# Another order of the attention's steps behind the load of pair 12, in an attention and soft-MoE kernel

## The chip, the cores and the metric

One core of a Trainium2 chip runs the whole kernel as one program. The metric is the device time of one execution in microseconds (us), the median of several runs. One execution was also taken by the hardware profiler; its rows are used below.

## The reference

Inputs are q, k, v of 4 batches x 8 heads x 768 positions x 64, and the weights of a soft mixture of experts (8 experts, 4 slots each, 1024 hidden).

```python
scores = scale * q @ k.T - slopes * dist          # per head, ALiBi distance
scores = where(is_global | is_local, scores, -1e9) # 8 global keys, window of 96
a = softmax(scores); x = (a @ v) -> [3072 tokens, 512]
logits = x @ phi                                   # 32 slots
d = softmax(logits over tokens); slot_input = d.T @ x
slot_out[e] = relu(slot_input[e] @ w1[e]) @ w2[e]
c = softmax(logits over slots); out = c @ slot_out
```

## The kernel before

**Units.** The attention is done in 16 units u = 0 to 15, each a pair of heads (i = 0, 1) of one batch; four units make a batch. A unit's 768 positions are cut into 7 blocks of 120 keys; scores are held as keys by queries, with 216 queries a block. Everything of the attention is written as named steps, and the list `ORDER` (L55) names them in the order in which they are put into the program; `steps` (L888) maps names to functions. Each engine runs its own steps in the order of that list, and waits where a step's input, or the buffer it writes, isn't ready. So a change of `ORDER` changes each engine's queue and nothing else in the work.

**The steps of unit u**, with engine and line:
- `load_qk` (L424), `load_v` (L427): transfers, issued on SP. q and k of a unit go to `raw` (u % 2), v to half of `vt` (u % 2), so a load waits until unit u-2 has been read.
- `scores u k`, k = 0 to 2, on PE (L571), into one of two `sc` PSUM tiles; `biased u k` on VectorE (L580) adds the bias table, keeps a running maximum, and writes `tb` (u % 3).
- `max_t` (PE, L587) and `max_r` (VectorE, L592) make the maximum over the keys; `exponential u i` on ScalarE (L596).
- The weights are split into two f16 parts: `w_hi u i` on ScalarE (L599) writes the high part to `ph`; `w_lo u i part`, three parts, on GpSimd (L606), or `w_lo_dve` on VectorE, the rest. v is split the same way: `v_hi` on GpSimd (L539), `v_hi_act` on ScalarE (L542) or `v_hi_dve` on VectorE (L545), then `v_lo` on VectorE (L549).
- `values u i` on PE (L623): 39 f16 matmuls of 65 columns; the parts of `w_lo` are needed one after the other, the last one by the last 16 matmuls. It waits until the PSUM tile `x` of unit u-1 has been read.
- `ev_sums`, `ev_recs`, `ev_mul u i` on VectorE (L639, L645, L651): normalise into `xn`, of which there are three buffers, one for each two units. (The last unit has them head by head: `ev_sum`, `ev_rec`, L632, L636.)
- `tr u k` on PE (L663) transposes `xn`; `tr_copy u k` on ScalarE (L668) or `tr_copy_dve` on VectorE (L672) copies it out, 480 columns for k = 0 and 288 for k = 1; `logits u` on PE (L693) takes two units. `max_t`, `tr`, `logits`, `by_token` and `dispatch` share a ring of two PSUM banks.
- At the end of a batch: `logits_all` (VectorE, L710), `strip_max`, `strip_exp`, `strip_sum` (a running softmax over tokens: L727, L734 to L738, L744, L746), `by_token` (PE, L751), its copies (ScalarE, L764, L768), `dispatch` (PE, L774: 28 matmuls on `xn`), `dispatch_sum` (VectorE, L785).

**Weights.** The expert weights are 32 pieces of 1024 KB. Ten go to places of their own (`piece`, L413). Thirteen go to buffers of the attention, each of which is loaded by `free i` (L418) once its last reader in the attention is done. Which piece goes to which buffer follows from the order of the `free` steps in `ORDER` (`held`, L380 to L384); so does the order in which the nine `extra` steps, early in `ORDER`, load the unused ends of these buffers. One piece goes to `spot`; the last eight go to the first places again, in column halves, as the tail's first matmuls release them (L949 to L957). Up to eight transfers are under way at a time, issued in order.

**The tail.** Behind `ORDER`, `last_dispatch` (L802) finishes the softmax over tokens of the last batch, starting from `logits_all 15`; then the hidden layer (L104), the projections (L159) and the combination (L205) follow on PE, and copies (L218) and transfers bring the output out.

Of the kernel before, what the change touches and what calls it, by code (L numbers as in the profile page):

```python
# [28 lines left out]
QW = KB + WIN  # L29
# [278 lines left out]
def tile_attention_moe(ctx: ExitStack, tc: tile.TileContext, qk, v, phi, w1, w2, nn, out):  # L308
    nc = tc.nc
# [58 lines left out]
    phi_ = [t[:, 0:PH].bitcast(F16) for t in pht]  # L368
# [11 lines left out]
    held = []  # L380
    for name, i, *_ in ORDER:
        if name == "free":
# [70 lines left out]
    def blocks(w):  # L453
        return w[:, 0:6 * PB].rearrange("p (s c) -> p s c", c=PB)
# [19 lines left out]
    def late_constants():  # L474
        nc.gpsimd.tensor_tensor(out=i4, in0=ident[:, 0:32], in1=ident[:, 32:64], op=ALU.add)
        nc.gpsimd.tensor_tensor(out=i4, in0=i4, in1=ident[:, 64:96], op=ALU.add)
        nc.gpsimd.tensor_tensor(out=i4, in0=i4, in1=ident[:, 96:128], op=ALU.add)
        nc.gpsimd.tensor_copy(out=by_row.rearrange("p (s j) -> p s j", s=4), in_=ident.rearrange("p (s r) -> p s r", s=4)[:, :, 0:NS // 4])
        nc.gpsimd.memset(sl, 0.0)
        moe.constants()  # L480
# [18 lines left out]
    def tb(u):  # L499
        return tbuf[u % 3]  # L500
# [53 lines left out]
    def warm_x(u):  # L554
        for n in (256, 256, P):
            nc.tensor.matmul(out=xx[:, 0, 0:n], lhsT=idb[:, 0:P], rhs=idb[:, 0:n], start=True, stop=True)
# [31 lines left out]

    def max_r(u):
        m = ms.pop((u, "m"))[:, 0:P]  # L590
        nbs[u] = nb = wk.tile([P, 1], F32, name="nb", tag="nb", bufs=2)
        nc.vector.tensor_tensor_reduce(out=m, in0=m, in1=shift.to_broadcast([P, P]), scale=-T_SC, scalar=3.0e38, op0=ALU.add, op1=ALU.min, accum_out=nb)  # L592

    def exponential(u, i):
        t = tb(u)[:, i]
        nc.scalar.activation(out=t, in_=t, func=AF.Exp, bias=nbs[u], scale=T_SC)  # L596

    def w_hi(u, i):
        nc.scalar.copy(out=blocks(phi_[i])[:, :, 0:QW], in_=tb(u)[:, i].rearrange("p (s c) -> p s c", c=QW))  # L599

    def w_hi_dve(u, i):
        nc.vector.tensor_copy(out=blocks(phi_[i])[:, :, 0:QW], in_=tb(u)[:, i].rearrange("p (s c) -> p s c", c=QW))

    def w_lo(u, i, part, engine=None):
        c = slice(2 * part, 2 * part + 2)
        (engine or nc.gpsimd).tensor_tensor(out=blocks(plo_[i])[:, c, 0:QW], in0=tb(u)[:, i].rearrange("p (s c) -> p s c", c=QW)[:, c],  # L606
                                            in1=blocks(phi_[i])[:, c, 0:QW], op=ALU.subtract)

    def w_lo_dve(u, i, part):
        w_lo(u, i, part, nc.vector)  # L610

    def values(u, i):
        ph, pl = phi_[i], plo_[i]
        vh, vl = vhi[u % 2], vlo[u % 2]
        x = sums(u, i)
        ops = []
        for t in range(NJ):
            for j, c in ((t, PCOL[t]), (t - 1, PCOL[t - 1] + KB)):
                if j >= 0:
                    for w, vv, d in ((ph, vh, D + 1), (ph, vl, D), (pl, vh, D + 1)):  # L620
                        ops.append((t, c, w, vv, j, d))
        for z, (t, c, w, vv, j, d) in enumerate(ops):
            nc.tensor.matmul(out=x[:, (D + 1) * t:(D + 1) * t + d], lhsT=w[:, c:c + P], rhs=vv[:, j, i, 0:d],  # L623
                             start=(z == 0), stop=(z == len(ops) - 1), skip_group_check=True)
# [253 lines left out]

    def table_rest_act(u):
        table.rest(nc.scalar.copy)  # L880

    def table_pair_act(p):
        table.pair_act(p)

    def table_pair(p):
        table.pair(p)

    steps = dict(piece=piece_of, free=free, extra=extra, load_phis=load_phis, bcast=bcast, keys=keys, table_rest=table_rest, table_rest_act=table_rest_act, table_pair_act=table_pair_act, warm_x=warm_x, warm=warm,  # L888
                 table_even=table_even, table_odd=table_odd, table_pair=table_pair, load_qk=load_qk, load_v=load_v, v_hi=v_hi, v_hi_act=v_hi_act, v_hi_dve=v_hi_dve, v_lo=v_lo,
                 scores=scores, biased=biased, max_t=max_t, max_r=max_r, exponential=exponential, w_hi=w_hi, w_lo=w_lo, w_lo_dve=w_lo_dve, w_hi_dve=w_hi_dve,  # L890
                 values=values, ev_sum=ev_sum, ev_rec=ev_rec, ev_sums=ev_sums, ev_recs=ev_recs, ev_mul=ev_mul, tr=tr, tr_copy=tr_copy, tr_copy_dve=tr_copy_dve,
                 logits=logits, logits2=logits2, logits_half=logits_half, logits_all=logits_all, strip_max=strip_max, strip_exp=strip_exp,
                 strip_sum=strip_sum, by_token=by_token, by_token_copy=by_token_copy, lnat_copy=lnat_copy, dispatch=dispatch, dispatch_sum=dispatch_sum)
    late_constants()
    for name, u, *args in ORDER:
        steps[name](u, *args)
    left = LeftBanks()
    put_rest = last_dispatch(left, lambda: warm_x(last))
    att.close()


    tail = ExitStack()
# [327 lines left out]
```

## Time and profile before

| | us |
|---|---|
| median of 3 runs | 185.19 |
| lowest and highest run | 184.1 to 185.4 |
| the profiled execution, its own time | 184.54 |
| its span, first to last instruction | 182.5 |

The span is what the profile's times count from. PE is TensorE's matmul row, PEld its weight-load row, DVE is VectorE, ACT ScalarE, POOL GpSimd, SP the engine that issues transfers. Matmuls overlap in the pipeline, so PE's busy time can hold some waiting. `<-` in brackets behind a row tells how long the engine was idle before it and what ended that.

### The profile page before, as it was taken

What the parts mean: (1) busy time and instruction counts of PE and PEld (TensorE: products, weight loads), DVE (VectorE), ACT (ScalarE), POOL (GpSimd) and SP (SyncE); (2) the same over time, 40 slices, a digit from 0 to 9 for tenths busy, and PEclk for the clock granted to TensorE, in tenths of its full rate; (3) what the DMA queues carried; (4) which work ended last, traced back from release to release, by engine and by line L of the source; (5) the groups of instructions that cost most, each with busy time, mean ns of one, the idle gap of its engine ahead of it and who ended that gap; (6) DMA issues with size and microseconds to landing.
All of it is one profiled execution on the core that took longest, in us unless ns stands there. A gap on an engine that the chain in (4) does not pass through costs nothing.

```text
span 182.5 us, 6745 instructions
## 1 busy us (share of the span) xinstructions
PE 170.5 (93%) x2805; PEld 125.8 (69%) x2805; DVE 141.6 (78%) x378; ACT 125.8 (69%) x164; POOL 97.2 (53%) x129
## 2 busy tenths in 40 slices
PE   8999899999999999999999998999899999999820
PEld 2567689797878877979888986875533256677710
DVE  5999999999998989899999999987867303346430
ACT  3499989999989999988999999953302120345320
POOL 6926689859799498797998996750010000000000
PEclk9999999999999999999999999999999999999975
DMA  6999999958998956789887399999999999989892
GB/s 186 420 399 390 413 400 392 392 192 307 381 391 338 383 156 247 250 310 379 288 344 276 89 310 376 407 370 416 416 387 409 408 404 404 380 303 405 347 334 65
DMA packets 15306, 61.41 MB, mean 337 GB/s; under 512 B 1698, under 2 KB 2850, under 8 KB 13474
## 3 DMA queue, kind: packets, MB, share of 16 engines
q1 hardware_dynamic: 15264, 60.89, 87.8%
q8 instruction: 24, 0.39, 0.9%
q14 instruction: 16, 0.13, 0.2%
q10 hardware_dynamic: 2, 0.00, 0.0%
HBM read 54.59 MB, written 6.29 MB: 334 GB/s over the span
## 4 chain that ended last, share of the span: by engine, by line


## 5 line engine op out<-in xcount | busy, mean ns | idle before, releaser
L606 POOL TENSOR_TENSOR ph<-tb,ph 128x432 f16<-128x432 f32 x83 | 85.9, 1066 | 18.9 <-ACT ph L599 15.8
L596 ACT ACTIVATE tb<-tb,nb 128x1296 f32<-128x1296 f32 x32 | 43.7, 1374 | 0.9 <-DVE nb L592 0.8
L623 PEld LDWEIGHTS <-ph 128*128 128x128 f16 x1248 | 40.7, 97 | 4.2 <-issue 2.8
L599 ACT CAST ph<-tb 128x1296 f16<-128x1296 f32 x32 | 40.6, 1271 | 2.8 <-PE x L623 0.9
L623 PE MATMUL x<-v,ph 128*128 128x65 f16 (+1 forms) x1209 | 42.0, 193 | 0.3 <-POOL ph L606 0.2
L571 PE MATMUL sc<-raw 64*128 64x216 f32 (+1 forms) x392 | 40.8, 340 | 0.0
L571 PEld LDWEIGHTS sc<-raw 64*128 64x128 f32 x392 | 32.3, 186 | 6.0 <-issue 3.5
L651 DVE CUSTOM_DVE_ANT_1 xn<-x,rc 120x448 f32<-120x448 f32 x31 | 18.3, 622 | 2.1 <-PE m L774 1.6
L580 DVE CUSTOM_DVE_ANT_1 tb<-sc,tt,mx 128x864 f32<-128x864 f32 x16 | 17.8, 1115 | 1.1 <-DVE mx L580 0.5
L549 DVE SCALAR_TENSOR_TENSOR v<-vt,v 128x896 f16<-128x896 f32 x14 | 16.2, 1159 | 0.0
L663 PE MATMUL m<-ident,xn 120*128 120x120 f32 x98 | 14.7, 276 | 0.2 <-DVE xmax L651 0.2
L663 PEld LDWEIGHTS m<-ident,xn 120*128 120x128 f32 x98 | 10.0, 141 | 2.7 <-issue 1.5
L104 PE MATMUL hp<-wp,sl 128*32 128x512 f32 x80 | 10.9, 594 | 0.3 <-ACT sl L99 0.3
L606 DVE TENSOR_TENSOR ph<-tb,ph 128x432 f16<-128x432 f32 x13 | 9.6, 765 | 0.0
L580 DVE CUSTOM_DVE_ANT_1 tb<-sc,xtt,mx 128x864 f32<-128x864 f32 x8 | 8.9, 1115 | 0.4 <-DVE mx L580 0.2
L580 DVE CUSTOM_DVE_ANT_1 tb<-sc,xta,mx 128x864 f32<-128x864 f32 x8 | 8.9, 1112 | 0.2
L542 ACT ACTIVATE v<-vt 128x896 f16<-128x896 f32 x9 | 8.6, 951 | 0.0
L205 PE MATMUL cp<-sos,ct 32*128 32x128 f32 (+1 forms) x120 | 8.4, 334 | 0.2 <-ACT ph L218 0.2
L159 PE MATMUL o<-wp,ht 128*32 128x128 f32 x256 | 8.4, 275 | 0.0
L580 DVE CUSTOM_DVE_ANT_1 tb<-sc,tt 128x864 f32<-128x864 f32 x8 | 8.4, 1050 | 0.0
L159 PEld LDWEIGHTS o<-wp,ht 128*32 128x32 f32 x256 | 6.6, 109 | 1.5 <-issue 1.0
L910 POOL MEMSET ht<- 128x536 f32 x1 | 0.5, 544 | 13.1 <-PE ld L848 13.1
(235 smaller groups left out, 283.5 us busy)
## 6 DMA issues: line engine op xcount, KB each, us to landing
raw<-in_qk_dram SPq DMA_DIRECT2D x14, 832.0 KB, 5.7
wp<-in_w_dram SPq DMA_DIRECT2D x10, 1024.0 KB, 8.0
wp<-in_w_dram SPq DMA_DIRECT2D x15, 512.0 KB, 9.0
vt<-in_v_dram SPq DMA_DIRECT2D x14, 448.0 KB, 5.5
tb<-in_w_dram SPq DMA_DIRECT2D x3, 1024.0 KB, 8.1
wp<-in_qk_dram SPq DMA_DIRECT2D x2, 832.0 KB, 9.5
raw<-in_w_dram SPq DMA_DIRECT2D x2, 832.0 KB, 4.5
ph<-in_w_dram SPq DMA_DIRECT2D x2, 768.0 KB, 9.9
```

The source lines that it names most:

```text
L104: self.nc.tensor.matmul(out=hp[n][32 * s:32 * s + 32, :], lhsT=slv(a, c, s), rhs=w1(4 * a + s, c // 2)[:, (c % 2) * DF + 512 * n:(c % 2) * ...
L159: nc.tensor.matmul(out=o[32 * s:32 * s + 32, o0:o0 + w], lhsT=ht[:, k:k + 32], rhs=w2(4 * a + s, half)[:, at:at + w], start=(a == 0 and c ...
L542: nc.scalar.activation(out=vhi[u % 2][:, :, :, 0:D], in_=vraws(u), func=AF.Copy, scale=V_SC)
L549: nc.vector.scalar_tensor_tensor(out=vlo[k].rearrange("p j i d -> p (j i) d"), in0=vraws(u).rearrange("p j i d -> p (j i) d"), scalar=V_SC ...
L571: nc.tensor.matmul(out=z[:, i, at:at + n], lhsT=r_[r, KCOL[j]:KCOL[j] + KR], rhs=r_[r, KW + KB * j:KW + KB * j + n], start=True, stop=True)
L580: nc.vector.tensor_tensor_reduce(out=tb(u)[:, :, BW * k:BW * k + BW], in0=sc[(3 * u + k) % 2][:, :, 0:BW], in1=table.unit(u % NP, k), scal ...
L596: nc.scalar.activation(out=t, in_=t, func=AF.Exp, bias=nbs[u], scale=T_SC)
L599: nc.scalar.copy(out=blocks(phi_[i])[:, :, 0:QW], in_=tb(u)[:, i].rearrange("p (s c) -> p s c", c=QW))
L606: (engine or nc.gpsimd).tensor_tensor(out=blocks(plo_[i])[:, c, 0:QW], in0=tb(u)[:, i].rearrange("p (s c) -> p s c", c=QW)[:, c], in1=bloc ...
L623: nc.tensor.matmul(out=x[:, (D + 1) * t:(D + 1) * t + d], lhsT=w[:, c:c + P], rhs=vv[:, j, i, 0:d], start=(z == 0), stop=(z == len(ops) - ...
L651: nc.vector.tensor_tensor_reduce(out=xnb[(u // 2) % 3][:, :, c:c + D], in0=by_query(u, i)[:, :, 0:D], in1=rcs.pop((u, i)).unsqueeze(2).to_ ...
L663: nc.tensor.transpose(out=m[:, at:at + KB], in_=xnb[(u // 2) % 3][:, t, P * (p % 2):P * (p % 2) + P], identity=ident[0:KB, 0:KB])
```

## The change

`ORDER` is the same up to and including `('load_qk', 12)`. Behind it the same 253 places hold another order. Each engine's queue changes as follows (steps that differ in kind or that the text speaks of; "..." where others are left out):

```diff
 steps that change engine
-('tr_copy', 9, 1), ('tr_copy', 10, 1), ('tr_copy', 13, 0)
+('tr_copy_dve', 9, 1), ('tr_copy_dve', 10, 1), ('tr_copy_dve', 13, 0)
-('v_hi_act', 14), ('v_hi', 15)
+('v_hi', 14), ('v_hi_dve', 15)
-w_lo_dve: (10,0,1), (12,0,2), (14,0,1), (14,0,2), (15,0,1), (15,0,0), (15,0,2)
+w_lo_dve: (10,0,2), (14,1,0), (14,0,0), (15,1,2), (15,0,1), (15,0,2)
 VectorE
-... v_lo 14, biased 15 2, ev_sums 13, ev_recs 13, ev_mul 13 0, max_r 15, ev_mul 13 1, strip_sum 3, logits_all 11, strip_max 11, tr_copy_dve 13 1, w_lo_dve 14 0 1, w_lo_dve 14 0 2, v_lo 15, ev_sums 14, ev_recs 14, tr_copy_dve 12 0, ev_mul 14 1, ev_mul 14 0, w_lo_dve 15 0 1, 15 0 0, 15 0 2, ev_sum 15 1 ...
+... biased 15 2, tr_copy_dve 11 1, v_lo 14, ev_sums 13, ev_recs 13, ev_mul 13 1, tr_copy_dve 10 1, w_lo_dve 14 1 0, max_r 15, ev_mul 13 0, logits_all 11, strip_max 11, w_lo_dve 14 0 0, v_hi_dve 15, tr_copy_dve 13 1, v_lo 15, w_lo_dve 15 1 2, ev_sums 14, tr_copy_dve 12 0, ev_recs 14, ev_mul 14 0, ev_mul 14 1, w_lo_dve 15 0 1, 15 0 2, tr_copy_dve 13 0, ev_sum 15 1 ...
-... ev_mul 15 0, strip_sum 7, strip_sum 11, tr_copy_dve 15 0, dispatch_sum 11, logits_all 15
+... ev_mul 15 0, tr_copy_dve 15 0, dispatch_sum 11, strip_sum 7, strip_sum 11, logits_all 15
 ScalarE
-... logits_half 9, v_hi_act 14, exponential 14 1, exponential 14 0, tr_copy 11 0, w_hi 14 1, tr_copy 10 0, tr_copy 10 1, w_hi 14 0, exponential 15 1 ...
+... logits_half 9, exponential 14 1, exponential 14 0, w_hi 14 1, tr_copy 11 0, tr_copy 10 0, w_hi 14 0, exponential 15 1 ...
 GpSimd
-... w_lo 12 0 0, 12 0 1, 13 1 0, 13 1 1, 13 1 2, 13 0 0, 13 0 2, 13 0 1, v_hi 15, w_lo 14 1 0, 14 1 1, 14 1 2, 14 0 0, 15 1 0, 15 1 2, 15 1 1
+... w_lo 12 0 1, 12 0 0, 12 0 2, 13 1 0, 13 1 1, 13 1 2, v_hi 14, w_lo 13 0 1, 13 0 0, 13 0 2, 14 1 1, 14 1 2, 14 0 2, 14 0 1, 15 1 1, 15 1 0, 15 0 0
 PE (the last fourteen steps, from by_token 11 on, are the same)
-... values 13 0, tr 10 0, tr 10 1, max_t 15, logits 11, tr 13 1, values 14 1, tr 12 1, by_token 11, values 14 0 ...
+... values 13 0, tr 10 0, tr 10 1, max_t 15, logits 11, tr 12 1, values 14 1, tr 13 1, by_token 11, values 14 0 ...
 SP
-load_qk 13, piece 9, load_v 12, load_qk 14, piece 8, load_v 13, load_qk 15, load_v 14
+load_qk 13, load_v 12, load_qk 14, piece 9, load_v 13, load_qk 15, load_v 14, piece 8
-free 0, load_v 15, free 14, 11, 1, 9, 3, 16, 4, 10, 7, 17, 6, 2, 8, 13, 5, 12, 15
+free 0, load_v 15, free 14, 11, 1, 3, 16, 9, 4, 10, 7, 17, 2, 8, 6, 15, 5, 13, 12
```

PE's 60 steps from there are the same steps; further pairs of them change places. From the order of the `free` steps it follows that the pieces 16 to 19, 21 and 22 go to other buffers (`tb0`, `v16`, `ph1`, `xtt`, `xta`, `tt` in place of `ph1`, `tb0`, `v16`, `xta`, `tt`, `xtt`), and that some of the early `extra` loads change places.

Beside it come functions that no step of `ORDER` calls:

```diff
+    def w_hi_part(u, i, part, copy=nc.scalar.copy):
+        c = slice(2 * part, 2 * part + 2)
+        copy(out=blocks(phi_[i])[:, c, 0:QW], in_=tb(u)[:, i].rearrange("p (s c) -> p s c", c=QW)[:, c])
+
+    def w_hi_part_dve(u, i, part):
+        w_hi_part(u, i, part, nc.vector.tensor_copy)
+
+    def w_hi_part_pool(u, i, part):
+        w_hi_part(u, i, part, nc.gpsimd.tensor_copy)
```

## Rows read from the trace of the kernel before

**Rows 1.** The page's first line.
```profile
span 182.5 us, 6745 instructions
```
**Rows 2.** View by stretches: length, busy of PE, PEld, DVE, ACT, POOL; clock, DMA share, GB/s.
```profile
112.00:119.00 7.00, 6.30 (x125) 5.06 (x128) 6.67 (x23) 6.77 (x12) 5.82 (x7) 1.00 1.03 400
76.90:127.20 50.30, 49.34 (x901) 40.72 (x898) 46.81 (x125) 43.93 (x57) 38.26 (x37) 1.00 0.88 324
```
**Rows 3.** Waits on PE's row, 76.9 to 127.2 us: total, times, longest.
```profile
PE m L587 <- ACT xtt L668: 0.4, 1, 0.4
...
PE x L623 <- POOL ph L606: 0.2, 1, 0.2
```
**Rows 4.** Timeline of VectorE from the dispatch to the last logits: start, length.
```profile
119.77 0.62 DVE L651 CUSTOM_DVE_ANT_1 xn<-x,rc 120x448 f32<-120x448 f32 x1 [0.77 <-PE m L774]
...
124.39 0.47 DVE L746 SCALAR_TENSOR_TENSOR state<-state,al 128x1 f32<-128x1 f32 x2
125.63 0.66 DVE L672 COPY xta<-x 128x480 f32<-128x480 f32 x1 [0.77 <-PE x L663]
126.20 0.74 DVE L785 SCALAR_TENSOR_TENSOR sacc<-sacc,al,m 128x512 f32<-128x512 f32 x1
127.14 0.40 DVE L710 CUSTOM_DVE_ANT_0 lsb<-sc,lsb 96x240 f32<-96x240 f32 x1 [0.21 <-PE sc L693]
```
**Rows 5.** View by stretches, the tail.
```profile
132.30:170.00 37.70, 37.68 (x620) 20.79 (x620) 16.17 (x41) 8.83 (x21) 0.54 (x1) 1.00 0.99 387
```
**Rows 6.** View of the tile `wp`, behind 130 us: issues (ns, first and last start), landing.
```profile
L413 SPq DMA_DIRECT2D wp<-in_w_dram x17: 327/328/1166, 135.0 to 151.6; - x17
...
DMA to landing us min/median/max: 8.1/9.1/11.0
```
**Rows 7.** Timeline of PE, start of the last projection.
```profile
164.84 1.08 PE L159 MATMUL o<-wp,ht 128*32 128x128 f32 x32
```
**Rows 8.** Groups by shape, 75 to 128 us: busy us, mean ns of one.
```profile
L549 DVE SCALAR_TENSOR_TENSOR v<-vt,v 128x896 f16<-128x896 f32 x7 | 8.4, 1199 | 0.0
...
L672 DVE COPY xta<-m 128x480 f32<-128x480 f32 x2 | 1.2, 623 | 0.0
...
L672 DVE COPY xtt<-m 128x288 f32<-128x288 f32 x2 | 0.9, 458 | 0.1
...
L542 ACT ACTIVATE v<-vt 128x896 f16<-128x896 f32 x4 | 3.8, 947 | 0.0
L668 ACT COPY xtt<-m 128x480 f32<-128x480 f32 x3 | 1.7, 560 | 0.8 <-PE m L663 0.8
```
**Rows 9.** Timeline of VectorE, single operations.
```profile
2.27 0.27 DVE L261 TENSOR_SCALAR xn<-xn 128x216 f32<-128x216 f32 x1
...
4.18 0.16 DVE L865 TENSOR_SCALAR nlt<-m 128x2 f32<-128x2 f32 x1 [0.74 <-PE m L861]
...
115.34 1.79 DVE L606 TENSOR_TENSOR ph<-tb,ph 128x432 f16<-128x432 f32 x2
...
120.87 1.64 DVE L606 TENSOR_TENSOR ph<-tb,ph 128x432 f16<-128x432 f32 x3
```
**Rows 10.** Timeline of GpSimd, PE and its weight loads around `values 13 0`, `values 14 1`.
```profile
102.74 6.79 POOL L606 TENSOR_TENSOR ph<-tb,ph 128x432 f16<-128x432 f32 x6 [0.23 <-ACT ph L599]
...
111.08 0.91 PE L663 MATMUL m<-ident,xn 120*128 120x120 f32 x7
...
112.23 3.91 POOL L606 TENSOR_TENSOR ph<-tb,ph 128x432 f16<-128x432 f32 x4
...
115.23 0.54 PEld L623 LDWEIGHTS <-ph 128*128 128x128 f16 x16 [0.25 <-POOL ph L606]
```
**Rows 11.** Timeline of SP: issue of piece 8, of load_v 14.
```profile
86.72 0.43 SPq L413 DMA_DIRECT2D wp<-in_w_dram  x1
...
97.80 0.33 SPq L427 DMA_DIRECT2D vt<-in_v_dram  x1
```
**Rows 12.** View by stretches, the hole in the transfers.
```profile
100.00:105.00 5.00, 5.00 (x109) 4.57 (x110) 4.85 (x8) 4.68 (x6) 4.77 (x5) 1.00 0.38 111
```

More of the change, by code (lines that the diff above doesn't have):

```diff
@@ L889, in tile_attention_moe @@
                  table_even=table_even, table_odd=table_odd, table_pair=table_pair, load_qk=load_qk, load_v=load_v, v_hi=v_hi, v_hi_act=v_hi_act, v_hi_dve=v_hi_dve, v_lo=v_lo,
-                 scores=scores, biased=biased, max_t=max_t, max_r=max_r, exponential=exponential, w_hi=w_hi, w_lo=w_lo, w_lo_dve=w_lo_dve, w_hi_dve=w_hi_dve,
+                 scores=scores, biased=biased, max_t=max_t, max_r=max_r, exponential=exponential, w_hi=w_hi, w_lo=w_lo, w_lo_dve=w_lo_dve, w_hi_dve=w_hi_dve, w_hi_part=w_hi_part, w_hi_part_dve=w_hi_part_dve, w_hi_part_pool=w_hi_part_pool,
                  values=values, ev_sum=ev_sum, ev_rec=ev_rec, ev_sums=ev_sums, ev_recs=ev_recs, ev_mul=ev_mul, tr=tr, tr_copy=tr_copy, tr_copy_dve=tr_copy_dve,
```

2 lines of the change are left out of this document (1 added, 1 removed).

## The prediction

> **What bounds the kernel now.** The page comes first, for the span and the whole [rows 1]; no single engine fills that span, and the chain of waits is empty in this profile, so the limit is read stage by stage, from the view by stretches. I cut it where the change acts: from 76.9 us, where VectorE starts the first step behind the shared prefix, to 127.2 us, where it starts `logits_all 15` [rows 2]. Of these 50.30 us PE is busy 49.34 (idle 0.96), VectorE 46.81 (idle 3.49), ScalarE 43.93, GpSimd 38.26. PE and VectorE are both nearly full; the other two wait for them. The table of waits confirms it from below: no wait on PE's own matmul row is longer than 0.4 us in this stretch, and none of those listed is for a transfer [rows 3].
>
> Next the end: of VectorE's last steps before the tail [rows 4] the final one, `logits_all 15` at 127.14, waits 0.21 us for PE's matmuls on `sc` (L693), so PE ends last there.
>
> Behind 127.2 us nothing of the change lies. From 132.3 to 170.0 us PE is busy 37.68 of 37.70 us [rows 5], so the tail follows the attention at a fixed distance, unless its weights come late. They don't: the last of the reused weight places is issued at 151.6 and the slowest landing takes 11.0 us, hence 162.6 at the latest [rows 6]. What is issued last are the second column halves; only the last projection reads them, from 164.84 on [rows 7]. That leaves over 2 us even at the slowest landing. The sum is thus: how much earlier or later does `logits_all 15` start than 127.14 us? The clock adds nothing: it is granted at 1.00 (2.4 GHz) in every stretch of rows 2.
>
> **The change part by part.** *Work per engine.* PE has the same 60 steps in another order. VectorE takes three transposes' copies and the last v conversion, and gives one correction part to GpSimd. Copies of 288 columns take 0.458 us, of 480 columns 0.623 [rows 8]; a correction part with no neighbour takes 1.64 / 3 = 0.55 [rows 9]. The conversion (`v_hi_dve`, 128x896) was never run on VectorE here. Below it lies the same operation at 216 columns, 0.27 us; above it the two-input operation at the same 896 columns, 1.20 us [rows 8, 9]. With a 2-column one at 0.16 us the slope is (0.27 - 0.16) / 214 = 0.51 ns a column, so I estimate 0.16 + 894 x 0.51 ns = 0.62 us, the operation's own kind being nearest. Sum on VectorE: 2 x 0.458 + 0.623 + 0.62 - 0.55 = +1.61 us (1.26 to 2.19). ScalarE loses these copies and `v_hi 14`, at most 0.95 + 3 x 0.56 = 2.63 us [rows 8]; it is idle 6.37 us of the stretch already [rows 2], so more idle time there buys nothing by itself.
>
> *Does VectorE have room?* Over the stretch yes, 3.49 against 1.61. Locally the tight place is 112 to 119 us, with 0.33 idle [rows 2]. There the new order puts in a 288 copy (0.458), the conversion (0.62) and three correction parts (1.65), and takes out two parts (1.79 as they ran, rows 9): +0.94. Less 0.33 that leaves 0.61 us, which falls on the 0.77 us in which VectorE waits for the dispatch matmuls before `ev_mul 14` [rows 4]. So it is hidden, and what is late next is PE's dispatch itself. If PE reaches the dispatch later by the same amount, the 0.61 comes out at the end.
>
> *GpSimd's queue.* `v_hi 14` and `w_lo 12 0 2` now stand in front of the three `w_lo 13 0` parts. Queued behind them are these parts, and `values 13 0` on PE waits for the parts; behind it in PE's queue stand `tr 10`, `max_t 15` and `logits 11`. GpSimd began the six parts of pair 13 at 102.74; eight instructions from there at 3.91 / 4 = 0.98 us end at 110.6. The last part is needed only by the last 16 of the 39 matmuls (0.54 us), hence 111.1 against 111.08, when PE began its next step before [rows 10]. Cost 0, up to 0.7 us if one meeting with VectorE (below) comes on top.
>
> *Meetings of VectorE and GpSimd.* Two correction parts on VectorE took 1.79 us beside GpSimd against 1.10 alone, so one meeting costs 0.69 [rows 9]. The operations that can meet number 14 before (7 `v_lo`, rows 8, and by the order 7 parts) and 14 after (7, 6 and the conversion). I take 0 and keep 0.69 both ways.
> The Trainium skill ("SBUF — State Buffer", section "Who interferes with whom") calls this an exclusive lock: whichever starts first holds the shared ports for its whole instruction. The 0.69 us agree. It also says that a one-input operation such as the conversion can take that lock in a two-port mode; no row here shows that, and by it the change could have one meeting of its own, 0.69 us more.
>
> *A wait that goes.* PE's 0.2 us wait for GpSimd [rows 3], in `values 14 1`, should go: ScalarE, relieved of `v_hi 14`, does `w_hi 14 1` ahead of `tr_copy 11 0`, and GpSimd does two parts of `14 1` instead of three. I count -0.2. The 0.4 us wait of `max_t 15` for ScalarE's copy stays, since a copy of tr 10 still stands before it.
>
> *A wait that comes.* `strip_sum 7` and `11` ran in a hole at 124.39, 0.47 us together; now they stand between `dispatch_sum 11` and `logits_all 15`. The first ends at 126.20 + 0.74 = 126.94, so `logits_all 15` can't start before 127.41: +0.27 [rows 4].
>
> *Transfers.* Piece 9 is issued behind load_v 12 and load_qk 14, piece 8 behind load_v 13, load_qk 15 and load_v 14: from 86.72 to behind 97.80 us [rows 11]. There it falls into a hole: the transfer engines are busy 0.38 of 100 to 105 us [rows 12]. The loads that were behind the two pieces come sooner, but no PE wait is for a load. Cost 0. The last spaces freed are re-ordered too, some issued 2 us sooner; with the slack above worth 0. The new helpers `w_hi_part*` are called by no step: 0.
>
> Sum: 184.54 (the profiled execution: the 182.5 us span and 2.0 around it) + 0.27 - 0.2 = 184.6. The profiled execution lies 0.65 under the median of the runs, 185.19; on the median's scale the forecast is 185.3 us, no change that can be told.
>
> **The rivals.** *Faster: the waits are packed away.* VectorE idles 3.49 us; if the new order fills all of it around its 1.61 us of new work, `logits_all` starts 1.88 us sooner: 185.19 - 1.88 = 183.3. For it: PE's weight loads are busy 40.72 of 50.30 us only, so PE's row may hold stalls that a better order removes. Against it: the matmul row's 0.96 us idle, and 1.54 us of VectorE's idle time is two waits for PE behind 119 us.
> The Trainium skill ("Perfetto Trace Analysis", section "Identifying the Most-Contended Engine") calls matmul busy time a bad measure of headroom and takes weight-load time instead: by that PE has 9.58 us of room and doesn't bound the gain, by the matmul row 0.96.
>
> *Slower: VectorE's queue sets the end.* If VectorE and not PE binds through 112 to 124 us, nothing hides its added work: 1.61 + 0.27 + one meeting 0.69 = 2.57, so 187.8 us. It begins to decide when `ev_mul 14` no longer waits for PE. For it: 0.33 us idle in 112 to 119. Against it: the two 0.77 us waits for PE behind.
>
> *The transfer part decides after all.* Piece 8 is 1024 KB; at the 387 GB/s of the tail (rows 5) it is 2.7 us. If the weights of the tail were the limit, work that the queue puts off would come out there: 187.9. Against it stands the slack; I give it little. That the re-ordering of the queue does what it is for, and that this is worth nothing because PE never waited for these weights, is inside my forecast.
>
> **How the numbers follow.** No change 0.66, faster 0.17, slower through VectorE 0.14, through the queue 0.03. One per cent is 1.85 us, about what a measurement of this kernel can tell from no change (the runs before spread over 1.3 us); it lies between the forecast and each rival. So 0.17 faster, 0.66 within 1%, 0.17 slower. The likeliest case's own range is 185.3 less PE's 0.96 idle, plus 0.61 + 0.69, so 184.3 to 186.6; both rivals have real weight, so the range reaches into each: 183.4 to 187.1.
>
> **What would show it.** Right: VectorE still waits for the dispatch before `ev_mul 14`; `logits_all 15` starts within 1 us of 127.14 with no wait for PE before it; PE idle up to it stays near 1 us; from there the tail's rows have the same distances. The wrong step would be the bound by PE, if PE's row has no more idle and the attention still ends over 1.8 us sooner; or the hole of 0.77, if it is gone and the end is later; or the slack, if PE waits for `wp` behind 156 us.

## The result and the profile after

| | before | after |
|---|---|---|
| median of 20 runs each, us | 184.87 | 186.15 |
| lowest to highest, us | 184.1 to 185.5 | 184.7 to 188.1 |
| the profiled execution, own time and span, us | 184.54, 182.5 | 185.33, 183.1 |

The ratio is 1.0064, with a 95% interval of 1.0039 to 1.0090: no change by the bound of 1% and inside the range, but 0.64% slower where 0.04% was forecast. The ratios, here and below, leave out runs more than 1.5% above the fastest of the same kernel (four of the twenty after, two of `compute_only`, one of `copy_back`), so the two medians above lie a little further apart, 1.28 us. So the question of the experiments is where 1.2 us come from that the sum did not have.

The page's first line of the kernel after, for [rows 1]:

```profile
span 183.1 us, 6740 instructions
```

The view by stretches of the kernel after: length, busy time of PE, PEld, DVE, ACT, POOL, then clock, DMA share and GB/s. The first line is the attention behind the shared prefix, up to `logits_all 15`, the second the tight place, the third the tail, for [rows 2, 5]:

```profile
77.43:128.32 50.89, 49.56 (x901) 40.73 (x898) 48.54 (x128) 42.11 (x53) 40.81 (x38) 1.00 0.90 327
112.00:119.00 7.00, 6.21 (x116) 4.88 (x114) 6.85 (x21) 6.00 (x11) 4.75 (x5) 1.00 1.01 388
133.47:171.17 37.70, 37.69 (x620) 20.82 (x620) 16.16 (x41) 8.82 (x21) 0.54 (x1) 1.00 0.98 381
```

VectorE has 1.73 us more work than in [rows 2] (48.54 against 46.81; forecast 1.61), the stretch is 0.59 us longer, and the tail is the same length as in [rows 5], only later.

*A start that varies.* Here everything lies 0.53 us later from the very first `biased` step on (7.69 us against 7.16), long before the orders differ, and a second profile of the same kernel has it at 7.17. Of the fourteen profiles of this study nine start at 7.16 to 7.30 and four at 7.59 to 7.81 (the fourteenth, `four_fewer`, comes below). The late starts arise on PE: six filler matmuls at 4.08 us take 2.04 us in the kernel before and 1.56 in the second profile, but 2.63 here; why they vary isn't shown. Times called "on a common start" have this difference taken off. On a common start `logits_all 15` begins at 127.79 in both profiles of the changed kernel, against 127.14: the attention really costs 0.65 us.

Four steps of VectorE in the kernel before, `v_lo 14`, `ev_sums 13`, `max_r 15` and `ev_sums 14`, then GpSimd's `v_hi 15` with the idle time in front of it:

```profile
109.92 1.08 DVE L549 SCALAR_TENSOR_TENSOR v<-vt,v 128x896 f16<-128x896 f32 x1
...
111.96 0.17 DVE L639 TENSOR_TENSOR rsall<-x,eps 120x14 f32<-120x14 f32 x1
...
112.99 0.29 DVE L592 CUSTOM_DVE_ANT_0 m<-m,shift 128x128 f32<-128x128 f32 x1
...
118.05 0.16 DVE L639 TENSOR_TENSOR rsall<-x,eps 120x14 f32<-120x14 f32 x1
```

```profile
111.33 0.94 POOL L539 TENSOR_SCALAR v<-vt 128x896 f16<-128x896 f32 x1 [1.79 <-PE x L623]
```

The timeline of VectorE after (start, length, engine, line, operation, tiles, idle time before it and what ended that), for [rows 4]; take off 0.53 us to compare:

```profile
110.38 1.75 DVE L549 SCALAR_TENSOR_TENSOR v<-vt,v 128x896 f16<-128x896 f32 x1
112.05 0.16 DVE L649 TENSOR_TENSOR rsall<-x,eps 120x14 f32<-120x14 f32 x1
...
113.44 0.99 DVE L616 TENSOR_TENSOR ph<-tb,ph 128x432 f16<-128x432 f32 x1
114.36 0.28 DVE L592 CUSTOM_DVE_ANT_0 m<-m,shift 128x128 f32<-128x128 f32 x1
...
115.91 0.82 DVE L616 TENSOR_TENSOR ph<-tb,ph 128x432 f16<-128x432 f32 x1
116.65 0.62 DVE L545 TENSOR_SCALAR v<-vt 128x896 f16<-128x896 f32 x1
...
118.67 1.42 DVE L616 TENSOR_TENSOR ph<-tb,ph 128x432 f16<-128x432 f32 x1
120.02 0.16 DVE L649 TENSOR_TENSOR rsall<-x,eps 120x14 f32<-120x14 f32 x1
...
120.66 0.22 DVE L655 RECIPROCAL rc<-rsall 120x14 f32<-120x14 f32 x1
121.03 0.62 DVE L661 CUSTOM_DVE_ANT_1 xn<-x,rc 120x448 f32<-120x448 f32 x1
...
126.70 0.66 DVE L682 COPY xta<-x 128x480 f32<-128x480 f32 x1 [0.72 <-PE x L673]
127.28 0.74 DVE L795 SCALAR_TENSOR_TENSOR sacc<-sacc,al,m 128x512 f32<-128x512 f32 x1
127.93 0.47 DVE L756 SCALAR_TENSOR_TENSOR state<-state,al 128x1 f32<-128x1 f32 x2
128.32 0.40 DVE L720 CUSTOM_DVE_ANT_0 lsb<-sc,lsb 96x240 f32<-96x240 f32 x1
```

The conversion (L545) took 0.62 us, as estimated. But the three correction parts (L616) of this stretch took 0.99, 0.82 and 1.42 us where 0.55 each was put in, and `v_lo 14` (110.38) took 1.75 where it took 1.08 before. The reduction `max_r 15` (L592), which has the part at 113.44 in front of it, comes 0.84 us later than before on a common start. The row at 121.03, `ev_mul 14 0`, has no wait of 0.77 us before it any more. The 0.14 us that are left stand behind VectorE's own `ev_recs 14` (120.66), and are no wait for PE: before, the wait ended 1.55 us after the dispatch had begun (118.22 to 119.77), which here would be at 120.69.

Three steps on PE, first in the kernel before and then after; they are the first matmuls of `logits 11`, the dispatch, and `logits 13` (after, also the last 16 matmuls of `values 13 0`, then `tr 10`, and `tr 12 1` at 114.75):

```profile
112.66 0.40 PE L693 MATMUL m<-xtt,phis 128*32 128x240 f32 x5
...
118.22 1.93 PE L774 MATMUL m<-xn,dn 120*32 120x256 f32 x28
...
124.02 0.40 PE L693 MATMUL sc<-xta,phis 128*32 128x240 f32 x5
```

```profile
111.24 0.65 PE L633 MATMUL x<-v,ph 128*128 128x65 f16 x16 [0.16 <-POOL ph L616]
111.73 0.91 PE L673 MATMUL m<-ident,xn 120*128 120x120 f32 x7
...
113.58 0.40 PE L703 MATMUL m<-xtt,phis 128*32 128x240 f32 x5 [0.28 <-DVE xtt L682]
...
114.75 0.53 PE L673 MATMUL m<-ident,xn 120*128 120x120 f32 x3 [0.16 <-DVE nb L592]
...
119.14 1.93 PE L784 MATMUL m<-xn,dn 120*32 120x256 f32 x28
...
125.05 0.40 PE L703 MATMUL sc<-xta,phis 128*32 128x240 f32 x5
```

On a common start the three steps lie 0.39, 0.39 and 0.50 us later, and the last logits 0.65. So 0.39 of the 0.65 us are lost up to the dispatch. On the way there PE waits for GpSimd's last part for `values 13 0` (`tr 10` starts 0.12 us later than before, 111.20 against 111.08), for VectorE's copy of `tr 10 1`, then (L673) for `max_r 15`. In `values 14 1` it wins back 0.31 us and loses most of that again at `by_token 11`. That step needs ScalarE's `strip_exp 11`, which stands behind `exponential 15 1`, and this one waited for `max_r 15` too. Which wait sets the dispatch, `all_back` and `part_back_four_more` tell apart below.

### The profile page after: what moved, and what is told of

Read it like the earlier page. It is cut to its first block, busy times and chain, and to the rows that moved or that the text cites. A ratio compares the mean times of both kernels' runs of the same rounds, so it can differ in the third digit from the quotient of the medians.

```text
span 183.1 us, 6740 instructions
## 1 busy us (share of the span) xinstructions
PE 171.2 (93%) x2805; PEld 125.8 (69%) x2805; DVE 143.4 (78%) x381; ACT 124.0 (68%) x160; POOL 99.7 (54%) x130
## 4 chain that ended last, share of the span: by engine, by line
PE 66%; DVE 24%; issue 4%; POOL 1%; ACT 1%; DVEq 0%; POOLq 0%
PE sc L571 16%; PE x L633 14%; DVE tb L580 8%; PE hp L104 8%; PE o L159 4%; PE x L159 4%; PE m L673 4%; DVE v L549 3%; DVE xn L661 3%; DVE ph L616 3%; PE cp L205 2%; PE m L703 2%; PE m L784 2%; PE x L560 1%; PE x L205 1%
## 5 line engine op out<-in xcount | busy, mean ns | idle before, releaser
L616 POOL TENSOR_TENSOR ph<-tb,ph 128x432 f16<-128x432 f32 x84 | 88.4, 1083 | 19.4 <-ACT ph L599 18.2
L549 DVE SCALAR_TENSOR_TENSOR v<-vt,v 128x896 f16<-128x896 f32 x14 | 16.7, 1192 | 0.0
L673 PE MATMUL m<-ident,xn 120*128 120x120 f32 x98 | 14.6, 276 | 0.2 <-DVE nb L592 0.2
L673 PEld LDWEIGHTS m<-ident,xn 120*128 120x128 f32 x98 | 10.0, 141 | 2.6 <-DVE nb L592 0.6
L616 DVE TENSOR_TENSOR ph<-tb,ph 128x432 f16<-128x432 f32 x12 | 9.5, 803 | 0.0
L542 ACT ACTIVATE v<-vt 128x896 f16<-128x896 f32 x8 | 7.6, 953 | 0.0
```

Of the source, the lines that this page charges most:

```text
L549: nc.vector.scalar_tensor_tensor(out=vlo[k].rearrange("p j i d -> p (j i) d"), in0=vraws(u).rearrange("p j i d -> p (j i) d"), scalar=V_SC ...
L673: nc.tensor.transpose(out=m[:, at:at + KB], in_=xnb[(u // 2) % 3][:, t, P * (p % 2):P * (p % 2) + P], identity=ident[0:KB, 0:KB])
```

## The experiments

Times at `logits_all 15` are on a common start; before has 127.14.

| run | ratio to before (95%) | `logits_all 15` |
|---|---|---|
| after_again | 1.0080 (1.0051 to 1.0109) | 127.79 |
| compute_only | 1.0032 (1.0006 to 1.0058) | 127.78 |
| transfers_only | 0.9984 (0.9968 to 0.9999) | 127.14 |
| placement_only | 0.9981 (0.9964 to 0.9998) | 127.16 |
| conversion_back | 1.0084 (1.0045 to 1.0124) | 128.21 |
| copy_back | 1.0094 (1.0064 to 1.0124) | 127.58 |
| all_back | 1.0062 (1.0028 to 1.0096) | 127.67 |
| gpsimd_room | 1.0094 (1.0061 to 1.0126) | 127.89 |
| room_copy_strip | 1.0072 (1.0045 to 1.0100) | 127.56 |
| part_back_four_more | 1.0069 (1.0047 to 1.0090) | 128.34 |
| four_more | 1.0050 (1.0031 to 1.0070) | 127.84 |
| four_fewer | 1.0090 (1.0057 to 1.0123) | 127.17 |

**Which part of the change costs it.** Three kernels split it, and the changed kernel ran once more beside them.

```diff
 compute_only: the changed order of PE, VectorE, ScalarE, GpSimd
-SP's queue and the places of the weights as changed
+SP's queue and the places of the weights as before
 transfers_only: the order of the four engines as before
+SP's queue and the places of the weights as changed
 placement_only: ORDER as before
+held = the changed order of places
```

> The new order of the four computing engines, with SP's queue (and with it the places of the weight pieces) as before the change. Theory 1, the computing order costs the time (VectorE's and GpSimd's queues from 112 us on): ratio to before 1.005 to 1.008, logits_all 15 about 0.6 us later against its own start, and the same wide spread of times as the changed kernel. Theory 2, the transfers' order or the places cost it: ratio 0.998 to 1.002 and a spread as narrow as before (1.4 us).

> The old order of the computing engines with SP's new queue (pieces 9 and 8 behind later loads, the last spaces re-ordered, the pieces 16 to 22 in other buffers). Theory 1: ratio 0.998 to 1.002, spread under 1.5 us. Theory 2: ratio 1.004 or more, and some executions over 186.7 us, by a load that lands late because piece 8 stands in front of load_v 15.

> The kernel before, with the weight pieces in the buffers of the changed kernel, so that only the places and the order of the early extra loads differ. Theory 1 and theory 2 in its form of SP's queue: ratio 0.998 to 1.002. If the places matter (the early extra loads or the output buffers): the start-up 0.5 us later at the first biased step in every profile, ratio about 1.003.

> The changed kernel once more beside the three others, for a second profile. All theories: ratio 1.004 to 1.009. If the 0.55 us by which its first profile ran late already before the first biased step is chance, this profile need not have it; if it belongs to the change, it has it again. Theory 1: VectorE's idle time before ev_mul 14 is under 0.3 us again and a correction part on VectorE takes over 1.2 us beside GpSimd.

`logits_all 15` answers without doubt: 127.78 with the computing order alone, 127.14 and 127.16 with the rest alone. The transfers' order and the places cost nothing, by the trace and by the time. Of the time the computing order alone shows a ratio of 1.0032, which is its 0.64 us (0.35%) and less than the 1.005 to 1.008 expected; the whole change shows more. Whether the transfers add something in the new order isn't settled by these runs, as the intervals of compute_only and after_again overlap.

**Taking single steps off VectorE.**

```diff
 conversion_back
-('v_hi_dve', 15)
+('v_hi', 15)
 copy_back
-('tr_copy_dve', 13, 0)
+('tr_copy', 13, 0)
 all_back: both, and
-('tr_copy_dve', 10, 1)
+('tr_copy', 10, 1)
-('dispatch_sum', 11), ('strip_sum', 7), ('strip_sum', 11), ('logits_all', 15)
+('strip_sum', 7), ('strip_sum', 11), ('tr_copy_dve', 15, 0), ('dispatch_sum', 11), ('logits_all', 15)
```

> The changed kernel, with the high part of v of unit 15 made by GpSimd again (v_hi 15) and not by VectorE; GpSimd stood idle 2.04 us before its first part of unit 15, so it has room. Theory, VectorE's queue from 112 to 125 us sets the end: the 0.62 us conversion goes out of it, so ev_mul 15 0 (124.83 in the second profile of the changed kernel) and logits_all 15 (127.79 there) start 0.5 to 0.65 us sooner, and the ratio falls by about 0.003. Rival, the new order of PE's own steps sets the end: logits_all 15 stays at 127.7 to 127.9 and the ratio stays.

> The changed kernel, with the 480-column copy of tr 13 0 on ScalarE again, which idles 3.57 us there. Theory, VectorE's queue sets the end: ev_sum 15 1 starts 0.57 us sooner (122.86 in place of 123.43) and logits_all 15 0.4 to 0.57 us sooner, the ratio falls by about 0.003. Rival, PE's own order sets the end: nothing moves at logits_all 15.

> The changed kernel with four of VectorE's additions undone: the conversion of v 15 on GpSimd, the copies of tr 13 0 and tr 10 1 on ScalarE, and the two strip sums back in the hole before the copy of tr 15 0. Theory, VectorE's queue sets the end: 0.62 + 0.57 + 0.37 + 0.10 = 1.66 us leave it, PE takes over as the limit on the way, and logits_all 15 starts at 126.3 to 127.1, no later than the 127.14 of the kernel before; ratio 0.995 to 1.001. Rival, PE's order: logits_all 15 at 127.6 or later and ratio above 1.003.

*conversion_back missed.* Its 128.21 holds 0.42 us that arise at `biased 7 1` (47.8 us), in the part that no edit touches; less that it is 127.79, a gain of nothing. The timeline of GpSimd in that kernel, then that of VectorE:

```profile
116.13 1.30 POOL L539 TENSOR_SCALAR v<-vt 128x896 f16<-128x896 f32 x1
```

```profile
115.80 0.82 DVE L616 TENSOR_TENSOR ph<-tb,ph 128x432 f16<-128x432 f32 x1
116.86 0.46 DVE L682 COPY xtt<-m 128x288 f32<-128x288 f32 x1 [0.23 <-PE m L673]
117.46 1.09 DVE L549 SCALAR_TENSOR_TENSOR v<-vt,v 128x896 f16<-128x896 f32 x1
```

On GpSimd the conversion took 1.30 us and was ready at 117.4, when VectorE had waited 0.23 us for PE and 0.14 us more (116.86 + 0.46 = 117.32, to 117.46). So `v_lo 15` starts only 0.11 us sooner than in the kernel after (117.46 - 0.42 against 117.68 - 0.53). The rest of the 0.62 us went into such waits, and the 0.11 didn't reach the end.

*copy_back* moved `ev_sum 15 1` by 0.53 of the 0.57 us expected (123.42 to 122.89), but only 0.21 came out. The timeline of VectorE in that kernel:

```profile
126.10 0.66 DVE L682 COPY xta<-x 128x480 f32<-128x480 f32 x1 [1.04 <-PE x L673]
```

The wait for PE before the copy of `tr 15 0` grew from 0.72 to 1.04 us. What did come out is PE's `logits 13`: in the kernel after it starts at 124.53 on a common start, 0.14 us behind the last matmul of `tr 14`, just when `ev_mul 15 1` on VectorE has ended (124.47); here it follows `tr 14` at once (124.36).

*all_back*: of its 127.67, 0.23 us again arise at `biased 7 1`; less that, 127.44. From the copy of `tr 15 0` to `logits_all 15` it takes 1.52 us in place of 1.62, so the strip sums behind `dispatch_sum 11` cost 0.10 us. The theory that VectorE's queue as such sets the end is refuted: 1.66 us less work there gave 0.35. These are 0.21 us for the copy of `tr 13 0` and 0.10 for the strip sums, nothing for the conversion, and 0.04 for the rest. The timeline of PE in that kernel, `tr 12 1` and the dispatch:

```profile
114.44 0.53 PE L673 MATMUL m<-ident,xn 120*128 120x120 f32 x3 [0.45 <-DVE nb L592]
...
118.82 1.93 PE L784 MATMUL m<-xn,dn 120*32 120x256 f32 x28
```

With the copy of `tr 10 1` on ScalarE `logits 11` comes 0.30 us sooner (112.98 - 0.23 against 113.58 - 0.53). But PE then waits 0.45 us for `max_r 15`, and the dispatch stays where it was (118.59 against 118.61). So the copy of `tr 10 1` does not set it.

**Where PE falls behind first.**

```diff
 gpsimd_room
-('v_hi', 14)
+('v_hi_act', 14), ('exponential', 14, 0)
 room_copy_strip: the same, with copy_back and the strip sums of all_back
 part_back_four_more: copies and strip sums of all_back, two matmuls of four_more, and
-('w_lo_dve', 14, 1, 0)
+('w_lo', 14, 1, 1), ('w_lo', 14, 1, 0), ('w_lo', 14, 1, 2)
```

> The changed kernel, with the high part of v of unit 14 made on ScalarE (v_hi_act 14, ahead of exponential 14 0) as in the kernel before, and not on GpSimd. In the changed kernel GpSimd works without a gap from 103.9 to 113.4 us, so v_lo 14 on VectorE runs beside it and takes 1.77 us; in the kernel before it falls into GpSimd's idle 1.79 us and takes 1.08. Theory, this meeting is where the loss starts: with GpSimd's queue 0.93 us shorter v_lo 14 takes 1.1 to 1.3 us, ev_sums 13 comes 0.4 to 0.7 us sooner (111.5 to about 111.0), PE no longer waits 0.28 us for the copy of tr 10 1 before logits 11, and logits_all 15 comes 0.2 to 0.4 us sooner (127.4 to 127.6 on a start of 7.16). Rival, ScalarE, 0.85 us later by this, takes over: w_hi 14 1 ends at 111.4, GpSimd's parts of 14 1 run 0.8 us later and meet VectorE there, and logits_all 15 stays at 127.7 or later.

> The same with two more of the changes undone that earlier runs priced: the copy of tr 13 0 on ScalarE (0.25 us at logits_all 15) and the two strip sums in the hole before the copy of tr 15 0 (0.10). Theory, the three causes are separate and add up: 127.79 - 0.3 - 0.25 - 0.10 = 127.1, level with the kernel before; by the time the output end adds 0 to 1.5 us as long as PE's code load lies beside the last issues, ratio 1.000 to 1.005. Rival, they share one chain, and the largest takes the others with it: logits_all 15 at 127.4 or later.

> The changed kernel with VectorE relieved at the place where PE first falls behind: the correction part 14 1 0 on GpSimd (which idles 2.04 us behind its parts of unit 14), the copies of tr 10 1 and tr 13 0 on ScalarE, the strip sums in the hole, and the two small early matmuls that bring PE's stream to its old length. Theory, max_r 15 is late (113.82 against 112.98) because VectorE has a part and a copy in front of it, and PE's tr 12 1, then by_token and the dispatch wait for what follows from it: without the part max_r 15 starts at 112.8 to 113.1, tr 12 1 at 113.6 to 113.9 in place of 114.22, the dispatch at 118.0 to 118.3 in place of 118.60, and logits_all 15 at 126.8 to 127.2, level with the kernel before; the output end is as before (last issue within 1.8 us of PE's end), ratio 0.998 to 1.002. Rival, PE's new order or GpSimd's longer queue sets the dispatch: it stays at 118.5 or later, logits_all 15 at 127.4 or later, ratio 1.002 to 1.006.

*gpsimd_room*: the timeline of VectorE, then of PE:

```profile
109.93 1.08 DVE L549 SCALAR_TENSOR_TENSOR v<-vt,v 128x896 f16<-128x896 f32 x1
...
112.75 0.46 DVE L682 COPY xtt<-m 128x288 f32<-128x288 f32 x1 [0.51 <-PE m L673]
```

```profile
112.19 0.53 PE L673 MATMUL m<-ident,xn 120*128 120x120 f32 x3 [0.65 <-ACT tt L678]
...
113.27 0.40 PE L703 MATMUL m<-xtt,phis 128*32 128x240 f32 x5 [0.29 <-DVE xtt L682]
```

The meeting is gone, as the theory said (`v_lo 14` 1.08 us), and `ev_sums 13` is 0.44 us sooner. But PE now waits 0.65 us for ScalarE's copy, VectorE 0.51 us for PE, and the last logits are 0.10 us later: the rival. *room_copy_strip* at 127.56 lies where the rival had it, but not for the rival's reason: the prices as measured do add up (127.79 + 0.10 - 0.21 - 0.10 = 127.58). What failed is the 0.3 us that the theory gave to the meeting.

*part_back_four_more* confirmed the first half and lost it again. `max_r 15` came at 112.84, `tr 12 1` at 113.72 and the dispatch at 118.33, near the 118.22 of before. In `all_back`, where `logits 11` starts at the same time within 0.03 us but the part still stands in front of `max_r 15`, the dispatch came at 118.59; so 0.26 of the 0.39 us lost at the dispatch are this part's. But GpSimd now works from 110.32 to 117.38 without a gap. The timelines of GpSimd, VectorE and PE in that kernel (its start is 0.65 us late):

```profile
110.32 7.06 POOL L619 TENSOR_TENSOR ph<-tb,ph 128x432 f16<-128x432 f32 x6
```

```profile
115.35 1.17 DVE L619 TENSOR_TENSOR ph<-tb,ph 128x432 f16<-128x432 f32 x1
116.44 1.43 DVE L545 TENSOR_SCALAR v<-vt 128x896 f16<-128x896 f32 x1
...
118.28 1.70 DVE L549 SCALAR_TENSOR_TENSOR v<-vt,v 128x896 f16<-128x896 f32 x1
```

```profile
122.01 0.63 PE L676 MATMUL m<-ident,xn 120*128 120x120 f32 x4 [1.11 <-DVE xta L685]
```

The conversion takes 1.43 us beside GpSimd, 0.62 in the kernel after; the part 1.17 and `v_lo 15` 1.70 in place of 0.82 and 1.08. That is 1.78 us, and PE waits 1.11 us for VectorE's copy of `tr 12 0`. Each of these versions moves the loss between VectorE, GpSimd and ScalarE; none beats the kernel before. No run takes off the part, the copy of `tr 13 0` and the strip sums without filling GpSimd; that the three make up nearly all of the 0.65 us is the sum of their prices, 0.26 + 0.21 + 0.10 = 0.57.

**The end of the program.** 0.65 us in the attention is 0.35%, and the ratio is 0.64%. The rest is looked for behind the last matmul. The timeline of SP in the kernel before, and in the second profile of the kernel after: each row is the issue of two output transfers, with the time from the first's start to the second's end.

```profile
172.87 1.26 SPq L221 DMA_DIRECT2D out_dram<-xtt  x2
...
175.22 1.38 SPq L221 DMA_DIRECT2D out_dram<-tb  x2
```

```profile
173.51 1.95 SPq L221 DMA_DIRECT2D out_dram<-tt  x2
...
176.54 2.10 SPq L221 DMA_DIRECT2D out_dram<-v  x2
```

A pair takes 0.8 to 1.0 us undisturbed, a single issue mostly 0.33 to 0.4. The long ones stand beside a packet of the queue that the profile calls "q8 instruction", 24 packets of 16 KB in the whole program: in the fourteen profiles every issue of an output that takes 0.95 us or more overlaps one. The last of these packets that starts ahead of PE's end is called the load from here on. The view of transfers in the kernel before, 171.5 to 172.6 us, and in the second profile after, 173.2 to 174.2 us (packets, MB, share):

```profile
q8 instruction: 1, 0.02, 6.8%
```

```profile
q8 instruction: 1, 0.02, 9.8%
```

In the trace these two start at 172.07 and 173.52 us, 2.6 and 1.8 us ahead of PE's end. In the kernel before that is 0.8 us ahead of the pair, which takes 0.4 us longer than undisturbed; after it starts with the pair, which takes 1.1 us longer. PE's queue holds 40 semaphore instructions of its own in the new order, 44 in the old: four fewer. Two runs test whether that shifts the load.

```diff
 four_more, in the changed kernel, behind warm(0, 6):
+for _ in range(2):
+    nc.tensor.matmul(out=xx[0:1, 0, 0:16], lhsT=busy_in[:, 0:1], rhs=busy_in[:, 0:16], start=True, stop=True)
 four_fewer, in the kernel before:
-WARM = 6
+WARM = 4
```

> The changed kernel with two more small matmuls (16 columns) early, beside the first six that only keep PE busy: four more PE instructions, by which its instruction stream is as long again as before (it lacks four). For the end of the program: in the profiles with the new order of computing PE's next to last 16 KB code load starts 0.8 to 1.8 us later against the tail's work than in those with the old one, and the last output issues on SP that fall beside it take 1.0 to 1.8 us instead of 0.35. Theory, this place of the code load is why the median lies 1.3 us above before where the attention ends only 0.64 later: the load goes back to about 1.0 us ahead of the last copies, the last output is issued within 2.2 us of PE's end as in the kernel before, and the ratio falls to 1.003 to 1.005. Rival, the end varies by chance or by something else: ratio 1.006 to 1.009 as in the changed kernel.

> The kernel before, with two of the first six filler matmuls left out (nothing reads them): four PE instructions fewer, so that its PE stream is as long as the changed kernel's, with all of its work as before. Theory, the place of PE's code load against the tail stretches the last output issues: the next to last load comes 0.8 to 1.8 us later against the tail's work (after 172.8 instead of 172.1 on a start of 7.16), an issue of 1.0 us or longer falls behind 173.5, the last issue is at 176.7 or later, and the ratio is 1.002 to 1.006, with a spread of the runs over 2 us. Rival, the end varies by chance: ratio 0.998 to 1.001 and the spread of before.

SP's rows in four_more, of the outputs before and of the same two outputs, then in four_fewer of the same two:

```profile
172.45 1.82 SPq L221 DMA_DIRECT2D out_dram<-xta  x2
174.37 0.87 SPq L221 DMA_DIRECT2D out_dram<-tt  x2
```

```profile
173.96 1.91 SPq L221 DMA_DIRECT2D out_dram<-xtt  x2
```

four_more went by the theory: the load starts at 172.15 on a common start, the pair takes 0.87 us and the ratio falls to 1.0050. The load stretches the pair before instead (1.82 us). four_fewer went by it in part: the load starts at 172.95, the pair takes 1.91 us with all of the kernel's work as before, and the end lies 0.65 us later on a common start. But the last issue starts at 176.4 on that start, not at 176.7 or later, the six runs spread over 1.5 us and not over 2, and the ratio of 1.0090 is above the 1.002 to 1.006 expected. The rest of that ratio is its start, 1.06 us later; 0.68 of it are the next filler matmuls (first line before, second four_fewer). That leaving out the two caused this isn't shown: in part_back_four_more, which has them, the same row took 2.72 us too.

```profile
4.08 2.04 PE L560 MATMUL x<-const-bfloat16-1.0 128*1 128x512 bf16 x6
```

```profile
4.07 2.72 PE L560 MATMUL x<-const-bfloat16-1.0 128*1 128x512 bf16 x6
```

In all fourteen profiles the place of the load goes with the length of PE's stream. The five with the long one have the load 2.6 to 3.2 us ahead of PE's end, and from that end to the end of the span it takes 7.9, 8.1, 8.1, 8.0 and 7.9 us (before: 182.5 - 173.87 - 0.76). The nine with four instructions fewer have it 0.7 to 1.8 us ahead, and take 8.1, 7.3, 9.1, 9.1, 8.7, 9.9, 8.4, 7.8 and 8.5 us. The means are 8.0 and 8.55 us: 0.57 us, and with more spread, so that three of the nine end no later than the five. In eight of the nine the packet behind the load meets one of the last two pairs as well (an issue of 0.9 to 1.8 us); in the five no issue of these pairs takes over 0.93.

The times alone point the same way. Take each kernel's median of all runs, less that of the kernel before beside it, less what its attention costs: in the eight runs of the new order with the short stream 0.0 to 1.35 us are left, 0.8 in the mean, and in the four kernels with the long stream -0.5 to 0.3, -0.1 in the mean. These four spread over 1.3 to 1.6 us, the changed kernel over 3.4. One run speaks against it: compute_only has the short stream and its load 0.7 us ahead of PE's end, and its median holds nothing beyond the attention.

The Trainium skill ("Runtime: NRT & Kernel Launch", section "Instruction fetch mechanics") says that an engine's code is refilled in blocks of 16 KiB, or 256 instructions, and that the cost of crossing into the next one is mostly hidden. The size agrees with the packets here, and PE shows no cost: from `logits_all 15` to its last matmul it takes 47.5 us in both kernels. What these runs show beside it is a cost to another engine: an output's issue on SP takes 1.0 to 1.8 us beside such a packet, mostly 0.33 to 0.4 without.

The two parts give 0.65 + 0.57 = 1.22 us. The ratio of 1.0064 is 1.18 us (0.72 to 1.66). The interval of four_more overlaps that of the changed kernel, so the second part rests on the traces and on the medians together more than on this one ratio. That the sum comes so near is partly chance, as the second part scatters by over 2 us from profile to profile. Why four instructions shift the load by 0.8 to 1.8 us is not settled; that a wait of PE in the combination lies between the old and the new place of the boundary is only a guess.

## Why the prediction was right or wrong

The forecast was no change, 185.3 us in a range of 183.4 to 187.1; 186.15 and 0.64% fall into it, on the slower side. (Its base, 185.19 from three runs, lay 0.32 above the median of twenty.) That it fits is partly luck. The range left room for a cover that fails and for a meeting, which is near to what came in the attention; but by the two parts above nearly half of the loss arose at the end of the program, which stands in no term. Its steps:

- *Tail, transfers.* Right. PE waits for no weight in the tail, which kept its length; SP's queue and the places alone gave 0.998. *The bound by PE* held only in part: PE is idle 1.33 us in place of 0.96, and single steps of VectorE set when it runs.
- *Work on VectorE.* Right in the total, +1.73 us against +1.61, and the conversion took 0.62 to the digit. But the total holds about 0.7 us of meetings, which the sum had at 0 (six `v_lo` took 7.8 us, before 7.3; six correction parts 5.4, before seven 5.7), and about as much was saved where steps follow each other more closely. So that it agrees is partly luck.
- *"So it is hidden", 112 to 119 us.* Wrong, and this is the step that failed. From `ev_sums 13` to `ev_sums 14` VectorE takes 7.97 us, before 6.10: 1.87 us more, where the working had 0.94 less 0.33, so 0.61. The hole of 0.77 before `ev_mul 14` is gone and the end is later, which the prediction itself had named as the sign that this step is wrong. More than the size, the reasoning was wrong: the hole is a cover only for work that PE doesn't need. `max_r 15` stands in the same queue behind the added part `14 1 0` and feeds PE's way to the dispatch, which came 0.39 us later; 0.26 of that went with the part (part_back_four_more beside all_back). The prediction named that condition ("if PE reaches the dispatch later by the same amount") and did not look up which of VectorE's steps PE waits for.
- *Meetings, taken as 0.* Mis-sized. Counting the operations that can meet, 14 and 14, said nothing: GpSimd lost the idle 1.79 us in which `v_lo 14` had run. That alone is 0.67 us, and the parts at 113.44, 115.91 and 118.67 have 0.44, 0.27 and 0.87 over 0.55. What these meetings are worth at the end isn't shown: without that of `v_lo 14` the last logits came 0.10 us later (gpsimd_room).
- *GpSimd's queue.* Nearly right: forecast was the end of `values 13 0` at 111.1 us; PE waited 0.16 us for the last part, and the next step began at 111.20 on a common start, 0.12 later than before. The "up to 0.7 us" did not come.
- *The wait that goes, -0.2.* It went: `values 14 1` takes 1.34 us, before 1.65. PE lost most of that again at `by_token 11`.
- *Strip sums, +0.27.* Measured 0.10. The sum set 0.74 and 0.47 us end to end; from start to start the two rows took 0.65 and 0.39 (127.28, 127.93, 128.32).
- *Not in the sum.* `logits 13` waiting for `ev_mul 15 1`, 0.2 us (copy_back); and the end of the program, 0.57 us, which the prediction took as a fixed distance behind the attention.
- *The rivals.* The slower one, VectorE's queue as the bound, came true in its sign, since `ev_mul 14` no longer waits for PE, but not in its price: 2.57 us were put on the end and 0.65 came there, and all_back got 0.35 us from 1.66. Single steps of that queue set the end, not its length. The faster one never appeared: PE's idle time rose from 0.96 to 1.33 us.

## What to carry to other kernels

A hole in an engine's timeline covers added work only if the steps between the work and the hole feed nobody else; follow each of them to its reader before counting the hole. Where two engines disturb each other, count the idle time in which their operations run undisturbed now, and ask what will fill it. Behind a fixed tail the end can still move: look at what SP and the code loads do in the last 10 us.

## What the runs showed of the hardware that was not expected

- A one-input conversion on VectorE meets GpSimd as well: 0.62 us in the kernel after, 1.43 beside a running part (part_back_four_more). This agrees with what the Trainium skill ("SBUF — State Buffer", section "Who interferes with whom") says of such operations in a two-port mode, which no row of the kernel before had shown.
- The order of steps changes the number of PE's semaphore instructions (44 before, 40 after). With four PE instructions more or fewer another of the last outputs' issues meets a 16 KB packet: the same pair took 0.87 us in four_more and 1.91 in four_fewer.
- The same program repeats its computing times to about 0.03 us in the two profiles of the changed kernel; what varies over all profiles are the start (7.16 to 7.81 us), one step at 47.8 us (by 0.42 and 0.23 in two of fourteen), and the end.
